# One explicit order for the first 640 steps of a fused windowed-attention and FFN kernel

## The chip, the cores and the metric

The kernel runs on one core of one Trainium2 chip. The metric is device microseconds of one execution, from start to end. Three runs of the kernel before were made, and the median counts. Below, TensorE is PE in the profile's rows (its weight loads are PEld), VectorE is DVE, ScalarE is ACT, GpSimd is POOL and SyncE is SP. A `q` behind a name (SPq, ACTq) means that the engine's queue issued a DMA.

## The reference

Attention with a window of 64 positions over 8 batches, 8 heads, 576 positions of 64 dimensions; its output, as 4608 tokens of 512 numbers, goes through a two-layer network with a leaky rectifier. All in float32.

```python
scores = scale * np.matmul(q, k.transpose(0, 1, 3, 2))
rel = pos[:, None] - pos[None, :]
mask = (rel >= 0) & (rel < window)
scores = np.where(mask, scores, -1000000000.0)
scores = scores - np.max(scores, axis=-1, keepdims=True)
attn = np.exp(scores)
attn = attn / (np.sum(attn, axis=-1, keepdims=True) + 1e-09)
...
h = x @ w_in
g = np.maximum(0.01 * h, h)
return (g @ w_out).astype(np.float32)
```

## The kernel before, in words

Tokens are cut into 9 chunks of 512. Each chunk is 8 units of 64 queries, and two units (one `m`) go through attention together. Products that need full precision are made of three fp32r matmuls: a high and a low part of each operand, without low times low. The first three chunks go through the network as plain matrix products, the other six in three pairs of chunks by a scheme with seven products in place of eight.

The program is one long list of small steps. Each engine executes its own instructions in the order in which the steps were emitted (lines 1514 to 1523 pin that order), and waits at each instruction until its operands are there and its output buffer is free. So the emission order is the order of every queue.

Before the change the emission order has two parts. **ORDER** (line 141) names 514 steps of the head: chunk 0 and most of chunk 1 with the attention they need, and the preparation of weight tiles 0 to 28. They are emitted at once by lines 617 to 619. Then the rest of the kernel is written as a plan, `plan`, of 2303 numbered steps (`op`, line 625), and `arrange` (line 643) emits them in the order of **PLACES** (line 62). A name in ORDER is a kind and a number; `acts`, in front of `step` (line 613), says which function it calls:

- Attention of `m`, or of its half `b` = 2m or 2m+1: `q`, `k`, `v` load from HBM on SP. `S` makes the scores on TensorE (line 369; with the mask, line 403, for all but m = 0), `Z` adds the mask behind S0. `E` copies scores from PSUM to SBUF (line 413 on VectorE for b = 0 and 1, line 415 on ScalarE for the others), `P` takes the maximum over partitions on POOL (line 423, about 2 us), `N` (TensorE, line 437, b < 4) or `sub` (VectorE, line 428) subtracts it, `exp` follows on ScalarE (lines 442 and 444). `V` multiplies by the values (TensorE, line 458), `sm`, `rec` and `y` (VectorE, lines 465, 470, 477) divide by the sum. `T` turns the pair of halves (TensorE, line 484), `H` and `L` split it into high and low part (ScalarE, line 488, and VectorE, line 492).
- Weight half tile `n` (an even n is w_in, an odd one w_out, of tile n // 2): `raw` loads it (SP for n < 3, else the ACT queue), into one of 3 buffers. `bits`, `sign`, `clamp`, `join` on VectorE (lines 317, 321, 329, 334) and `abs` on ScalarE (line 325, between sign and clamp) make it a float32 in one of 2 buffers `w`; `chi` (ScalarE, line 337) makes the high part and issues its store to `w_single` on the ACT queue (line 338); `rest` (VectorE, line 342) makes the low part.
- FFN job `n`: `M` is the first product (TensorE, line 522), `lk` and `gh` the rectifier and the high part (ScalarE, lines 527 and 532), `gl` the low part (VectorE, line 536), `W` the second product (TensorE, line 558). Jobs 0 to 5 are on half a chunk, 256 columns; the others on 512. `ev` copies sums out.
- `X` with a number issues that many dummy 128x512 matmuls on TensorE (`idle`, line 591).

Of the plan's numbers that stand among the first steps: 30 and 31, 44 and 45, 51 and 52 are the first product of later jobs (`early_first`, line 1028), 53 to 56 a second product (`early_second`), 43, 50, 61 its VectorE step `low_of`, 38 to 40 the three stores of weight tile 6 and 46 to 91 other such stores (`store`, line 588, on SP), 149, 164, 179 scores of later `m`, 152 to 170 their POOL reductions.

Around 350 us, in code outside the changed lists, the seven-product stage prepares sums of weights and stores them to `w_sums` from the ACT queue (line 1162); rows below show one ScalarE wait for such a store.

Of the kernel before, what the change touches and what calls it, by code (L numbers as in the profile page):

```python
# [61 lines left out]
PLACES = """  # L62
30 1 7 40 0 38 39 5 2 31 3 10 32 17 41 42 43 44 13 33 34 4 6 45 35 36 9 51 8 12 11 14 15 52 48 16 18 23 49 53 19 59 20 149 50 22 54 21 162
25 55 24 26 56 27 62 28 60 29 63 37 521 46 150 520 61 152 64 69 151 57 65 47 66 155 67 73 153 154 156 164 70 158 71 74 531 165 177 72 530
75 80 522 81 524 76 157 166 167 159 77 68 78 525 523 84 160 526 85 163 82 527 86 91 87 83 170 161 529 88 58 528 89 168 179 532 169 534 173
95 202 181 92 180 96 171 533 172 97 102 182 93 101 98 174 192 535 99 94 536 197 175 193 194 541 540 103 100 537 106 104 185 198 176 105
538 107 183 222 539 108 186 117 184 196 109 178 188 195 204 114 110 206 226 111 205 119 115 543 189 210 217 120 542 544 218 207 116 121
219 127 118 122 187 545 211 203 123 551 190 124 546 130 550 128 131 547 208 191 132 549 199 133 209 134 129 548 220 213 212 221 228 140
146 136 141 135 138 275 142 229 200 143 552 276 147 139 231 137 241 214 554 277 283 555 553 278 251 215 230 556 279 148 280 561 242 246
243 560 223 232 216 234 286 145 227 112 224 557 284 287 235 245 201 288 294 244 289 225 559 233 290 285 271 237 291 247 297 558 295 253  # L70
562 266 236 564 565 298 267 239 603 296 268 238 255 299 125 305 254 300 563 301 566 302 256 240 308 306 567 570 252 309 307 259 571 568
248 310 569 316 257 269 605 270 260 258 79 311 249 607 262 261 312 627 313 319 317 618 318 320 264 606 263 581 619 620 321 327 322 580 250
323 272 324 265 608 273 315 330 572 573 331 611 609 332 341 274 304 333 610 126 612 328 623 343 614 329 622 613 344 621 334 303 624 574
# [123 lines left out]
def band_attention_ffn(ctx: ExitStack, tc: tile.TileContext, qk, vW, vL, w_in, w_out, eye_mask, out, outT):  # L197
# [413 lines left out]
    nc.scalar.copy(unit, eye_in)  # L611

    def step(name):
        kind = name.rstrip("0123456789")
        return partial(acts[kind], int(name[len(kind) :]))

    order, late = ORDER.split("|")
    for name in order.split():
        step(name)()
    prev = jobs[-1]  # L620


    plan = []
# [952 lines left out]
```

## Time and profile before

| what | us |
|---|---|
| median of 3 runs | 841.18 |
| lowest and highest | 840.93, 842.61 |
| span of the profiled execution | 841.2 |
| TensorE busy in it | 829.1 |
| VectorE busy | 630.8 |
| POOL busy | 381.5 |
| ScalarE busy | 369.7 |

The profiled execution is one more run of the same program; the trace gives its own time as the span, 841.2 us from the first to the last instruction. The profile says of each engine when it was busy, and of each idle stretch which other instruction or DMA ended it. A busy TensorE is not TensorE at its peak: matmuls overlap, so a step's cost is read from the distance of starts or from a group's whole time, not from the mean of one matmul.

### The profile page before, as it was taken

How to read it: one execution, taken by the hardware profiler on the slowest of the kernel's cores; microseconds unless marked ns; L12 is line 12 of the kernel's file. 1: busy time of each engine (PE TensorE's matmuls, PEld its weight loads, DVE VectorE, ACT ScalarE, POOL GpSimd, SP SyncE). 2: the span in 40 equal slices, each digit the busy share in tenths (PEclk: the TensorE clock that was granted, in tenths of full speed). 3: DMA queues.
4: the chain of work that ended last, by engine and by line, in shares of the span. 5: the costliest groups of instructions: out<-in, count | busy, mean ns of one | idle time of the engine just before them, and what ended most of it. 6: DMA issues, size and time to landing. Idle time of an engine off the chain costs nothing.

```text
span 841.2 us, 16743 instructions
## 1 busy us (share of the span) xinstructions
PE 829.1 (99%) x6733; PEld 678.1 (81%) x6733; DVE 630.8 (75%) x912; ACT 369.7 (44%) x599; POOL 381.5 (45%) x216
## 2 busy tenths in 40 slices
PE   8999999999999999989999999999999999999997
PEld 5777888888888888868888888887888888888886
DVE  6999897777766698667888987559799863366773
ACT  4666555344423355243564442233545422325432
POOL 5332000897867747687672116797941111111110
PEclk9999999999999999999999999999999999999999
DMA  9886866987887899999999798899998996677772
GB/s 327 278 276 209 310 223 225 319 287 259 277 295 251 271 342 379 365 299 359 361 321 308 224 316 251 255 282 241 261 278 243 317 257 184 190 197 200 212 200 89
DMA packets 131005, 225.75 MB, mean 268 GB/s; under 512 B 15856, under 2 KB 53744, under 8 KB 130928
## 3 DMA queue, kind: packets, MB, share of 16 engines
q0 software_dynamic: 53568, 88.09, 38.8%
q10 hardware_dynamic: 36608, 78.26, 27.6%
q1 hardware_dynamic: 40752, 58.34, 21.7%
q8 instruction: 53, 0.87, 0.4%
q14 instruction: 24, 0.20, 0.1%
HBM read 167.28 MB, written 57.26 MB: 267 GB/s over the span
## 4 chain that ended last, share of the span: by engine, by line
PE 89%; DMA 5%; DVE 3%; issue 1%; ACT 1%; POOL 0%; DVEq 0%; ACTq 0%
PE z L1309 27%; PE m L1243 25%; PE acc L1047 11%; PE h L1038 11%; PE acc L558 4%; PE s L369 4%; PE h L522 4%; PE o L829 3%; DMA w_sums<-pspare 2%; DMA qk<-qk 1%; DMA raw<-w_in 1%; DMA raw<-w_out 1%; DMA w_single<-w 1%; PE o L458 0%; DVE raw L321 0%
## 5 line engine op out<-in xcount | busy, mean ns | idle before, releaser
L1243 PE MATMUL m<-pfew,p 128*128 128x512 f32 x720 | 171.6, 394 | 3.0 <-ACT pxa L1249 2.5
L1243 PEld LDWEIGHTS m<-pfew,p 128*128 128x128 f32 x720 | 135.5, 189 | 32.5 <-ACT pxa L1249 2.9
L1309 PE MATMUL z<-gs,p 128*128 128x512 f32 (+1 forms) x360 | 86.0, 387 | 0.0
L1047 PE MATMUL acc<-p,gs 128*128 128x512 f32 x324 | 80.7, 393 | 0.0
L1309 PE MATMUL z<-pxa,p 128*128 128x512 f32 x324 | 78.5, 391 | 0.0
L1309 PEld LDWEIGHTS z<-gs,p 128*128 128x128 f32 x360 | 67.3, 188 | 13.9
L1309 PE MATMUL z<-pspare,p 128*128 128x512 f32 x324 | 78.0, 389 | 0.0
L1252 DVE TENSOR_TENSOR pxa<-m,pxa 128x512 f32<-128x512 f32 x60 | 41.2, 688 | 48.5 <-PE m L1243 43.6
L770 POOL PARTITION_ALL_REDUCE g<-late_f x20 | 36.3, 1842 | 86.6 <-DVE late_f L755 71.5
L1227 POOL DMA_DIRECT2D p<-w_first x42 | 31.7, 755 | 93.7 <-PE m L1243 51.6
L1309 PEld LDWEIGHTS z<-pspare,p 128*128 128x128 f32 x324 | 60.7, 188 | 12.6
L1309 PEld LDWEIGHTS z<-pxa,p 128*128 128x128 f32 x324 | 60.5, 188 | 12.9 <-issue 0.2
L1243 PE MATMUL m<-pxb,p 128*128 128x512 f32 x288 | 70.6, 391 | 0.0
L1047 PEld LDWEIGHTS acc<-p,gs 128*128 128x128 f32 x324 | 60.0, 188 | 12.8
L773 POOL PARTITION_ALL_REDUCE late_o<-late_f x20 | 65.2, 3274 | 9.6 <-ACT late_f L781 7.4
L773 POOL PARTITION_ALL_REDUCE late_o<-e x18 | 61.5, 3432 | 16.6 <-issue 7.9
L1252 DVE TENSOR_TENSOR p<-m,pxa 128x512 f32<-128x512 f32 x60 | 40.7, 687 | 36.6 <-PE m L1243 35.9
L773 POOL PARTITION_ALL_REDUCE late_o<-late_e x18 | 59.3, 3321 | 10.6 <-ACT late_e L781 6.0
L1243 PEld LDWEIGHTS m<-pxb,p 128*128 128x128 f32 x288 | 53.8, 188 | 11.4
L1227 POOL DMA_DIRECT2D p<-w_sums x24 | 18.0, 749 | 93.1 <-PE z L1309 76.8
L1038 PE MATMUL h<-pxa,p 128*128 128x512 f32 x228 | 55.9, 392 | 0.0
L1038 PEld LDWEIGHTS h<-pxa,p 128*128 128x128 f32 x228 | 42.4, 188 | 9.0
(201 smaller groups left out, 1600.5 us busy)
## 6 DMA issues: line engine op xcount, KB each, us to landing
p<-w_first POOLq DMA_DIRECT2D x42, 1024.0 KB, 7.0
p<-w_sums POOLq DMA_DIRECT2D x24, 1024.0 KB, 6.7
p<-w_second POOLq DMA_DIRECT2D x18, 1024.0 KB, 6.9
qk<-qk ACTq DMA_DIRECT2D x26, 512.0 KB, 6.2
w_single<-w ACTq DMA_DIRECT2D x32, 256.0 KB, 3.7
raw<-w_out ACTq DMA_DIRECT2D x15, 512.0 KB, 4.5
raw<-w_in ACTq DMA_DIRECT2D x14, 512.0 KB, 4.3
more_v<-vL ACTq DMA_DIRECT2D x14, 512.0 KB, 6.0
```

The costliest lines, as they stand in the source:

```text
L369: nc.tensor.matmul(ps[j][t, c : c + QB], k[i][s, p], q[s, w, p], start=not begun and (not more or (w, p) == (0, 0)), stop=not begun and no ...
L522: nc.tensor.matmul(ps, a[:, k, :], b[:, k, part], start=n == 0, stop=n == len(terms) - 1)
L558: nc.tensor.matmul(acc[c, i], a[:, ts], b, start=begin and n == 0, stop=end and n == 2)
L770: nc.gpsimd.partition_all_reduce(most_of(j), e_of(m)[:, j], P, ReduceOp.max)
L773: nc.gpsimd.partition_all_reduce(sum_of(j), e_of(m)[:, j], P, ReduceOp.add)
L829: nc.tensor.matmul(ps[64 * j : 64 * j + 64, c : c + QB], v[:, 2 * p + j], e_of(m)[:, j, c : c + QB], start=True, stop=True,)
L1038: nc.tensor.matmul(ps, a[:, k, :], b[:, k], start=i == 0, stop=i == len(terms) - 1)
L1047: nc.tensor.matmul(acc[c, i], a[:, i * P : (i + 1) * P], b, start=begin and k == 0, stop=n in ends and k == 2)
L1227: nc.gpsimd.dma_start(to, of, max_dma_last_dim=2048)
L1243: nc.tensor.matmul(tiles[b], w[:, 256 * i + 128 * kt : 256 * i + 128 * kt + 128], x_part(OF_X[k], j, kt), start=begin and c == 0, stop=c = ...
L1252: nc.vector.tensor_tensor(to(), tiles[b], x(), ALU.add)
L1309: nc.tensor.matmul(tiles[b + i][:, cut], a, x[:, cut], start=begin and f == first and c == 0, stop=f == half - 1 and c == 2, skip_group_ch ...
```

## The change

PLACES goes. ORDER now holds all 2817 steps, head steps by name and plan steps by number, and `arrange` emits both kinds in that order. The first 640 steps (up to about 170 us of the profile before) stand in a new order; the rest is the order of before. Every step is there once, as it was. The two bookkeeping edits (`turns_late` for `turns`, `room_of` for `more`) keep buffers the same now that head steps are emitted after the plan is written. The steps beyond the common point are cut from the diff.

```diff
--- before.py
+++ after.py
...
-PLACES = """
-30 1 7 40 0 38 39 5 2 31 3 10 32 17 41 42 43 44 13 33 34 4 6 45 35 36 9 51 8 12 11 14 15 52 48 16 18 23 49 53 19 59 20 149 50 22 54 21 162
...
+ORDER = """
+raw0 X6 q1 X2 X1 X2 S0 E1 k1 raw1 E0 Z1 P1 Z0 bits0 S1 sign0 N1 abs0 v0 clamp0 E2 q2 bits1 sign1 P0 join0 exp1 N0 exp0 abs1 P2 E3 clamp1
+k2 raw2 V1 V0 v1 join1 S2 sm0 chi0 sm1 E4 k3 N2 rec1 P3 exp2 y1 raw3 N3 rec0 q3 bits2 sign2 chi1 y0 rest0 T0 exp3 E5 rest1 P4 V2 sm2 V3 v2
+sub4 rec2 raw4 y2 H0 v3 P5 exp4 sm3 rec3 y3 S3 abs2 L0 clamp2 k4 T1 join2 H1 sub5 bits3 sign3 V4 chi2 exp5 q4 L1 sm4 k5 E6 raw5 rec4 V5
+sm5 P6 v4 rec5 abs3 y4 E7 y5 M0 rest2 lk0 T2 gh0 bits4 sign4 q5 sub6 H2 P7 gl0 L2 clamp3 M1 exp6 join3 abs4 V6 clamp4 join4 lk1 gh1 raw6
+chi3 sub7 bits5 chi4 W0 rest4 sign5 S4 exp7 V7 sm6 E8 raw7 E9 M2 sm7 rec6 rec7 y6 y7 P8 abs5 gl1 rest3 lk2 T3 sub8 clamp5 W1 H3 exp8 P9 L3
+V8 gh2 join5 chi5 v5 bits6 sign6 M3 rest5 sub9 abs6 raw8 lk3 clamp6 S5 bits7 exp9 sm8 sign7 abs7 gh3 M4 gl2 q6 join6 raw9 clamp7 k6 W2 gl3
+join7 q7 E10 rec8 y8 bits8 chi6 lk4 chi7 W3 raw10 V9 gh4 rest7 P10 gl4 sm9 sign8 abs8 rest6 bits9 rec9 M5 clamp8 W4 join8 sign9 lk5 sub10
+gh5 raw11 M6 chi8 abs9 y9 bits10 gl5 exp10 sign10 rest8 lk6 E11 clamp9 join9 v6 T4 H4 L4 gh6 raw12 W5 P11 V10 sm10 abs10 bits11 sign11
+sub11 abs11 M7 S6 clamp10 chi9 k7 join10 exp11 clamp11 rec10 y10 gl6 raw13 chi10 E12 P12 lk7 rest9 V11 bits12 sm11 rec11 sign12 rest10
+join11 gh7 abs12 raw14 W6 E13 clamp12 sub12 M8 exp12 chi11 y11 gl7 T5 rest11 V12 join12 H5 W7 P13 sm12 sub13 lk8 bits13 rec12 L5 raw15 y12
+S7 chi12 exp13 sign13 gh8 rest12 abs13 bits14 sign14 E14 clamp13 join13 V13 abs14 bits15 M9 39 v7 gl8 clamp14 E15 chi13 sm13 P14 sub14 W8
+join14 rec13 raw16 lk9 gh9 chi14 y13 raw17 sign15 rest14 T6 exp14 rest13 V14 abs15 sm14 gl9 P15 rec14 H6 sub15 clamp15 exp15 y14 join15
+M10 chi15 bits16 raw18 V15 sign16 abs16 sm15 W9 lk10 L6 rest15 rec15 clamp16 q8 y15 gh10 gl10 bits17 join16 T7 sign17 W10 H7 raw19 chi16
+abs17 L7 M11 clamp17 bits18 join17 raw20 chi17 ev0 rest16 sign18 rest17 abs18 bits19 lk11 sign19 clamp18 join18 gh11 raw21 bits20 M12 gl11
+M13 q9 ev1 sign20 abs19 chi18 abs20 clamp19 rest18 lk12 clamp20 join19 gh12 raw22 gl12 join20 bits21 sign21 chi19 bits22 chi20 W11 W12
+raw23 abs21 rest19 lk13 sign22 gh13 clamp21 join21 M14 chi21 gl13 lk14 rest20 bits23 raw24 M15 gh14 sign23 W13 abs22 clamp22 gl14 lk15
+join22 rest21 M16 abs23 gh15 clamp23 chi22 bits24 sign24 rest22 abs24 join23 raw25 40 chi23 gl15 lk16 rest23 clamp24 W14 join24 bits25
+raw26 W15 gh16 raw27 bits26 sign25 M17 gl16 abs25 lk17 M18 clamp25 join25 chi24 bits27 chi25 gh17 30 sign27 sign26 abs26 rest25 rest24
+gl17 raw28 clamp26 join26 abs27 clamp27 lk18 31 38 join27 1 chi26 W16 W17 rest26 gh18 bits28 chi27 gl18 sign28 41 4 0 32 44 2 5 3 6 7 17
+42 10 8 k8 11 15 33 43 45 51 13 9 12 52 34 19 18 20 v8 14 22 35 48 59 36 21 53 49 24 16 23 26 54 55 56 149 50 28 60 25 29 27 62 37 150 63
+162 152 69 61 151 155 520 521 153 64 65 66 67 156 154 73 157 70 74 71 531 75 76 80 164 46 522 530 160 524 77 158 72 159 177 163 78 84 165
+166 170 525 57 167 523 85 81 68 82 526 91 47 86 161 87 83 527 528 58 88 179 168 529 89 532 169 534 173 95 202 181 92 180 96 171 533 172 97
+102 182 93 101 98 174 192 535 99 94 536 197 175 193 194 541 540 103 100 537 106 104 185 198 176 105 538 107 183 222 539 108 186 117 184
+196 109 178 188 195 204 114 110 206 226 111 205 119 115 543 189 210 217 120 542 544 218 207 116 121 219 127 118 122 187 545 211 203 123
...
-ORDER = """
-raw0 k1 X6 S0 q1 E1 X2 Z1 E0 bits0 sign0 Z0 P1 S1 abs0 v0 P0 raw1 clamp0 join0 N1 E3 bits1 exp1 N0 q2 P3 V1 exp0 sign1
-V0 k2 E2 P2 sm0 rec0 S2 sm1 abs1 rec1 chi0 E4 clamp1 N2 q4 rest0 v1 join1 q3 chi1 exp2 y1 y0 rest1 N3 raw2 T0 bits2
-exp3 P4 k3 sub4 V2 raw3 sm2 E5 sign2 H0 V3 abs2 sm3 rec2 P5 rec3 y2 L0 exp4 v2 clamp2 y3 sub5 join2 raw4 S3 X1 T1
-bits3 exp5 H1 V4 E6 V5 chi2 P6 sm4 v3 sign3 L1 sm5 rec4 X2 M0 rec5 y4 k5 y5 rest2 k4 E7 abs3 raw5 clamp3 lk0 bits4
-join3 gh0 T2 gl0 H2 sub6 sign4 L2 abs4 M1 P7 W0 clamp4 exp6 join4 raw6 lk1 v4 S4 sub7 V6 bits5 chi4 exp7 rest4 sm6
-sign5 E8 V7 sm7 rec6 rec7 gh1 y6 chi3 q6 P8 abs5 y7 M2 raw7 gl1 T3 rest3 E9 q5 H3 W1 sub8 lk2 clamp5 exp8 L3 bits6 gh2
-join5 P9 raw8 gl2 chi5 V8 bits7 M3 sign6 rest5 lk3 abs6 gh3 S5 sign7 abs7 M4 clamp6 q7 v5 gl3 W2 join6 lk4 raw9 sub9
-clamp7 M5 bits8 exp9 join7 sign8 gh4 sm8 W3 rec8 E10 y8 chi6 P10 abs8 gl4 clamp8 chi7 rest6 raw10 lk5 sub10 V9 join8
-bits9 gh5 exp10 W4 v6 sm9 sign9 k6 rec9 gl5 M6 y9 T4 V10 chi8 rest8 abs9 raw11 lk6 rest7 bits10 clamp9 M7 gh6 H4 sm10
-sign10 E11 join9 W5 abs10 chi9 rec10 L4 y10 clamp10 bits11 join10 P11 sub11 S6 gl6 raw12 rest9 exp11 sign11 chi10 V11
-E12 raw13 rest10 abs11 lk7 sm11 gh7 rec11 P12 y11 W6 E13 T5 clamp11 bits12 join11 sign12 abs12 H5 raw14 gl7 bits13 k7
-sub12 clamp12 exp12 L5 join12 sign13 M8 chi11 chi12 W7 lk8 P13 rest11 raw15 rest12 sub13 bits14 abs13 S7 clamp13 V12
-sign14 join13 sm12 exp13 rec12 y12 E14 gh8 q9 abs14 M9 gl8 clamp14 v7 V13 W8 P14 raw16 bits15 sub14 join14 sm13 rec13
-lk9 y13 E15 chi14 exp14 chi13 rest14 sign15 T6 rest13 raw17 V14 gh9 P15 sm14 sub15 abs15 clamp15 H6 M10 rec14 gl9
-exp15 y14 k8 join15 L6 bits16 V15 W9 sm15 lk10 sign16 raw18 rec15 chi15 rest15 gh10 y15 T7 gl10 abs16 H7 clamp16
-join16 W10 bits17 L7 M11 raw19 sign17 M12 bits18 abs17 chi16 ev0 clamp17 join17 sign18 raw20 bits19 abs18 lk11 chi17
-sign19 rest16 gh11 clamp18 join18 v8 gl11 bits20 chi18 rest17 raw21 ev1 sign20 lk12 rest18 abs19 clamp19 join19 bits21
-gh12 gl12 M13 W11 raw22 abs20 M14 chi19 lk13 sign21 clamp20 abs21 gh13 W12 join20 gl13 clamp21 raw23 lk14 bits22
-sign22 rest19 chi20 gh14 rest20 M15 W13 abs22 join21 bits23 clamp22 raw24 chi21 sign23 join22 chi22 gl14 M16 raw25 W14
-abs23 rest21 bits24 sign24 lk15 clamp23 abs24 join23 gh15 rest22 gl15 bits25 clamp24 M17 sign25 chi23 raw26 lk16 gh16
-abs25 W15 join24 gl16 M18 chi24 clamp25 raw27 rest23 q8 bits26 sign26 abs26 lk17 join25 chi25 rest24 gh17 clamp26
-join26 gl17 bits27 sign27 raw28 abs27 chi26 W16 rest25 lk18 clamp27 join27 rest26 chi27 gh18 bits28 sign28 gl18 W17
-|
+LATE_WEIGHTS = """
 abs28 raw29 clamp28 join28 bits29 raw30 sign29 rest27 abs29 bits30 chi28 clamp29 sign30 rest28 abs30 join29 clamp30
 raw31 chi29 bits31 sign31 rest29 abs31 join30 clamp31 chi30 join31 rest30 chi31 rest31
 """
@@ -614,10 +610,8 @@
         kind = name.rstrip("0123456789")
         return partial(acts[kind], int(name[len(kind) :]))
 
-    order, late = ORDER.split("|")
-    for name in order.split():
-        step(name)()
     prev = jobs[-1]
+    turns_late = counter(len(jobs))
 
 
     plan = []
@@ -642,7 +636,11 @@
 
     def arrange():
         placed = set()
-        for n in map(int, PLACES.split()):
+        for word in ORDER.split():
+            if not word.isdigit():
+                yield step(word)
+                continue
+            n = int(word)
             assert placed.issuperset(a["n"] for a in plan[n]["after"])
             placed.add(n)
             yield plan[n]["fn"]
@@ -721,7 +719,7 @@
 
 
     weights_of, raw_of, single_of = {}, {}, {}
-    for name in late.split():
+    for name in LATE_WEIGHTS.split():
         kind = name.rstrip("0123456789")
         n = int(name[len(kind) :])
         o = weights_of.setdefault(n, {})
@@ -733,8 +731,8 @@
             "bits": ["raw"], "sign": ["bits"], "abs": ["sign"], "clamp": ["abs"], "join": ["clamp"], "chi": ["join"],
             "rest": ["chi"],
         }[kind]
-        more = [weights_of.get(n - 2, {}).get("rest")] if kind == "join" else []
-        o[kind] = op(engine, us, step(name), *(o.get(b) for b in before), *more, rank=0.3)
+        room_of = [weights_of.get(n - 2, {}).get("rest")] if kind == "join" else []
+        o[kind] = op(engine, us, step(name), *(o.get(b) for b in before), *room_of, rank=0.3)
     all_in = [weights_of[n][k] for n in (28, 29, 30, 31) for k in ("join", "rest")] + [weights_of[27]["rest"]]
     ready = {f: [weights_of.get(2 * f + i, {}).get("rest") for i in range(2)] for f in range(FT)}
 
@@ -1022,7 +1020,7 @@
     walk = [(c, half + k) for c in range(2) for k in range(half)] + [(2, f) for f in turn_of]
     opens = {n for n in range(len(walk)) if not n or walk[n][0] != walk[n - 1][0]}
     ends = {n for n in range(len(walk)) if n + 1 == len(walk) or walk[n][0] != walk[n + 1][0]}
-    pair_at = [pairs_of_g[next(turns) % 2] for _ in walk]
+    pair_at = [pairs_of_g[next(turns_late) % 2] for _ in walk]
     h_of, tiles, stage = {}, {}, {}
 
     def early_first(n, part):
```

The order on one engine is what is left when the other engines' names are struck out. For TensorE the lists begin so:

```
old: X6 S0 X2 Z1 Z0 S1 N1 N0 V1 V0 S2 N2 N3 T0 V2 V3 S3 X1 T1 V4 V5 X2 M0 T2 M1 W0 S4 V6 V7 M2 T3 W1 V8 M3 S5 M4 W2 M5 W3 V9 W4 M6 T4 V10 M7 W5 S6 V11 W6 T5 M8
new: X6 X2 X1 X2 S0 Z1 Z0 S1 N1 N0 V1 V0 S2 N2 N3 T0 V2 V3 S3 T1 V4 V5 M0 T2 M1 V6 W0 S4 V7 M2 T3 W1 V8 M3 S5 M4 W2 W3 V9 M5 W4 M6 T4 W5 V10 M7 S6 V11 W6 M8 T5
```

## Rows read from the trace of the kernel before

**Rows 1.** The page's first part: busy us (share of the span) and instructions by engine.
```profile
PE 829.1 (99%) x6733; PEld 678.1 (81%) x6733; DVE 630.8 (75%) x912; ACT 369.7 (44%) x599; POOL 381.5 (45%) x216
```

**Rows 2.** Five stretches (us): busy us (x instructions) by engine, TensorE's clock, DMA, GB/s.
```profile
4.60:24.53 19.93, 18.32 (x381) 12.02 (x382) 16.56 (x36) 11.29 (x22) 12.34 (x7) 1.00 0.98 358
24.53:60.00 35.47, 34.34 (x439) 28.20 (x439) 32.96 (x77) 22.64 (x45) 12.11 (x6) 1.00 0.85 272
60.00:357.00 297.00, 297.00 (x2736) 243.33 (x2736) 229.89 (x366) 136.21 (x240) 161.18 (x68) 1.00 0.86 286
357.00:361.00 4.00, 1.51 (x7) 0.90 (x6) 0.93 (x2) 2.14 (x4) 1.45 (x1) 0.95 1.17 368
360.70:364.00 3.30, 3.30 (x10) 2.53 (x9) 2.43 (x5) 2.64 (x5) 2.65 (x3) 0.50 0.64 217
```

**Rows 3.** Timeline of TensorE to 62 us: start, us, what, [idle before <-releaser].
```profile
1.45 2.93 PE L594 MATMUL idle<-p 128*128 128x512 f32 x6 [1.45 <-DVE p L605]
4.60 1.61 PE L369 MATMUL s<-qk 64*64 64x64 f32 x64 [0.22 <-DMA qk<-qk]
...
19.58 1.16 PE L369 MATMUL s<-p 64*64 64x64 f32 x64
...
21.87 0.63 PE L484 MATMUL t<-unit,y 128*128 128x128 f32 x4 [0.69 <-DVE y L477]
...
24.53 1.68 PE L522 MATMUL h<-pxa,pfew 128*128 128x256 f32 x12
...
52.14 0.63 PE L484 MATMUL t<-unit,y 128*128 128x128 f32 x4 [0.73 <-DVE y L477]
...
59.94 2.33 PE L558 MATMUL acc<-pfew,gs 128*128 128x512 f32 x9
```

**Rows 4.** Timeline of all engines to 27 us: VectorE and POOL at the start.
```profile
6.29 1.29 DVE L413 SCALAR_TENSOR_TENSOR e<-s,p 128x512 f32<-128x512 f32 x2 [4.90 <-PE s L369]
7.08 1.99 POOL L423 PARTITION_ALL_REDUCE p<-e  x1 [6.64 <-DVE e L413]
...
7.49 0.90 DVE L317 TENSOR_SCALAR raw<-raw 128x512 uint32<-128x512 uint32 x1
...
9.88 0.49 DVE L329 TENSOR_SCALAR raw<-raw 128x512 f32<-128x512 f32 x1 [0.75 <-ACT raw L325]
...
11.26 1.09 DVE L317 TENSOR_SCALAR raw<-raw 128x512 uint32<-128x512 uint32 x1 [0.16 <-DMA raw<-w_out]
...
13.64 0.16 DVE L465 TENSOR_SCALAR sm<-o 128x4 f32<-128x4 f32 x1 [0.57 <-PE o L458]
```

**Rows 5.** Who VectorE waited for to 100 us: us in total, times, longest.
```profile
DVE raw L317 <- DMA raw<-w_out: 4.2, 3, 2.7
...
DVE w L334 <- DMA w_single<-w: 0.9, 1, 0.9
```

**Rows 6.** Timeline of TensorE, 60 to 130 us.
```profile
77.94 0.69 PE L458 MATMUL o<-p,e 128*64 128x65 f32 x16
...
88.17 8.32 PE L522 MATMUL h<-pxb,pfew 128*128 128x512 f32 x36
```

**Rows 7.** Timeline of VectorE at 27 to 30 us, whose starts give the spacings.
```profile
27.46 0.42 DVE L536 TENSOR_TENSOR gs<-g,gs 128x256 fp32r<-128x256 f32 x1
27.80 0.68 DVE L428 TENSOR_TENSOR e<-e,g 128x512 f32<-128x512 f32 x1
28.40 0.69 DVE L321 SCALAR_TENSOR_TENSOR raw<-raw 128x512 uint32<-128x512 uint32 x1
...
29.83 0.43 DVE L329 TENSOR_SCALAR raw<-raw 128x512 f32<-128x512 f32 x1
```

**Rows 8.** Timeline of the SP queue: the issue of v7.
```profile
70.88 0.55 SPq L266 DMA_DIRECT2D p<-vW  x1
```

**Rows 9.** DMA issues to 100 us: count, KB each, median us to landing.
```profile
p<-vW SPq DMA_DIRECT2D x4, 520.0 KB, 6.3
```

**Rows 10.** Who ScalarE waited for between 350 and 361 us.
```profile
ACT late_f L761 <- DMA w_sums<-pspare: 8.5, 1, 8.5
```

## What the change will do to the time

> **What bounds the kernel now.** I began with the page's line of busy engines: TensorE is busy 829.1 of the span's 841.2 us [rows 1]. Only what TensorE waits for can move the end. Next came the table by stretches [rows 2]: in 4.60 to 24.53 TensorE is busy 18.32 of 19.93 us, in 24.53 to 60 it is busy 34.34 of 35.47, from 60 to 357 all 297.00. So the changed stretch (steps up to about 170 us) has 1.61 + 1.13 = 2.74 us of visible waiting, all of it before 60. After 60 nothing is to be had unless a new wait appears. The timeline of TensorE shows where the early waits lie [rows 3]: S0 starts at 4.60 on a load, T1 comes at 21.87 after 0.69 us on a `y`, M0 at 24.53, T4 at 52.14 after 0.73 on another `y`. The `y` come from VectorE, which is busy 32.96 of those 35.47 us [rows 2]: until 60 the kernel is bound by VectorE's order and TensorE's order together. VectorE itself waits where rows 4 show: 0.75 us for ScalarE before clamp0, 0.16 for a load before bits1, 0.57 for V0 before sm0; later 0.9 for a `w_single` store to land before join8, and 4.2 for three `w_out` loads [rows 5]. Of the 4.2, 0.16 is bits1's and 2.7 belongs to a load behind 60, so 1.3 is left, raw7's. The profile's own span, 841.2 us, stands at the median of the runs (841.18), so I add to that.
>
> **The change part by part.** The work is the same on every engine; only queues are reordered. Four of the moves matter.
>
> *Five dummy matmuls move to the front.* Old: X6, S0, X2, and later X1 before T1 and X2 before M0. New: X6 X2 X1 X2 all ahead of S0. The old ones stood inside waits (X2 ran while VectorE worked on E1, X1 ahead of T1's wait), so taking them out frees nothing. In front they stand in S0's way. Six take 2.93 us from 1.45 [rows 3], ending 4.38. The price of five more has two bounds: 0.23 each by the 36 matmuls of 8.32 us in rows 6, or 2.93 / 6 = 0.49 each. TensorE reaches its higher speed inside S0: S0's 64 small matmuls take 1.61 us, S3's take 1.16 [rows 3]. I take three at 2 x 0.23 and two at 0.23, 1.85 us less some overlap, 1.75: S0 begins at 6.1 where it began at 4.60, runs at full speed, 1.16 + 0.07, and E1 begins at 7.35 where it began at 6.29. That is +1.05 (bounds: start 5.5 to 6.8, so +0.5 to +1.8). The page's granted clock says 1.00 from the start, so this slow phase is read from durations alone.
>
> *VectorE's and ScalarE's order up to M0.* VectorE's work ahead of M0's last need (L1) is the same within one step: with the start-to-start spacings of rows 7 (0.60 for a step on 512 columns that is not a clamp or bits, 0.34 for those and for half-width ones, 0.33 for a `y`, 0.1 for `sm` and `rec`) I sum 13.6 us old and 13.5 new: 15 steps of 0.60, 7 of 0.34, 4 `y`, 8 or 9 small ones. What differs are waits. New: abs1 stands behind exp0 on ScalarE, and exp0 needs N0, N0 needs P0; POOL's two first reductions take about 1.99 us each, back to back behind E1 [rows 4], so they end near 12.1, N0 13.2, exp0 13.9, abs1 14.6, and clamp1 waits about 1.05 us for it. The old wait of 0.57 before sm0 goes, sm0 now comes after join1. rest1 waits about 0.7 for chi1 and clamp2 about 0.65 for abs2, both behind an exp on ScalarE. But L0 and clamp2 (0.94 us) moved from before y3 to behind it, so T1 still comes at about 22.1, against 21.87. Behind T1, clamp2, join2 and sub5 stand ahead of bits3 and L1: L1 ends at about 25.75, and M0 starts there, +1.2 against 24.53.
>
> One price here rests on POOL. bits0 takes 0.90 and bits1 1.09 us while POOL's reductions run [rows 4]; a clamp away from them takes 0.43 [rows 7]. I keep the long prices for the same two steps, since the reductions shift with them; each further step that comes to lie beside a reduction would cost 0.47 to 0.66 more (rival D). The Trainium skill ("GPSIMD Engine Reference", section 1, "Specifications") says that GpSimd shares its SBUF interfaces with VectorE and that VectorE instructions in a two-port mode or with two SBUF inputs contend with it. By that rule `rest` steps too could become long ones, and the sum would be D's; the trace agrees on bits0 and bits1.
>
> *From M0 to T4.* Both orders put the same VectorE steps ahead of sub7 (20.1 us), y7, gl1, sub8 and L3 (25.2 us by the spacings), so the lag stays what it is at M0: M2 comes near 34.4, W2 near 43.1. Then W3 and V9 run ahead of M5 in place of behind it, which moves no sum. T4 needs y9: 37.5 us of steps new, 37.2 old. The old T4 stood 0.73 us idle [rows 3], while VectorE had waited 1.3 us for raw7's load and 0.9 before join8 [rows 5]. raw7 is now issued right behind E8, where gh1, chi3 and abs5 stood between, so its wait goes; the one at join8 stays, as w6's store is issued about as much later. I get y9 at about 52.3 and TensorE ready at about 52.3. **The lag of 1.2 us has shrunk to about 0.2, as the old pauses before T4 are filled.**
>
> *From T4 to 60.* W5 now stands before V10. V11 needs y10 out of the same bank, which now stands behind clamp10, join10, clamp11 on VectorE; it lands near 59.3, V11 near 59.5. W6 needs gl6: 44.8 us of steps against 43.9, W6 near 60.2 where it was at 59.94. From there TensorE is full, as before. Sum: +0.3 us, 841.5.
>
> *The loads' queue.* Step 39 (a store of weight tile 6, waiting for rest12 on VectorE, near 70.6) now stands ahead of v7 on SP; v7 was issued at 70.88 behind q9 and is now issued near 71.1 [rows 8]. Its kind lands after 6.3 us [rows 9], so 77.4; V14 reads it at 77.94 old [rows 6], near 77.9 new. Price: nothing by that row, but with only 0.5 us to spare; a second store of the same queue ahead of it could cost up to 1 us. The other steps beyond it (W's and M's swapped with each other up to 128 us, plan steps by a few places up to 170) move where TensorE has whole stretches queued, 297.00 of 297.00 us [rows 2]. That queue is the cover; if it went, a swapped W would wait for its `gl`, 0.6 us each.
>
> **The rivals.**
>
> A, *slower by the clock*. Between 357 and 361 TensorE waits 2.49 us (busy 1.51 of 4.00), and the granted clock then stands at 0.50 from 360.7 to 364 [rows 2]: half of the 2.4 GHz level, 1.2. Without the X's ahead of T1 and M0, the new order leaves TensorE only V4 and V5 between T1 at 22.1 and M0 at 25.8, with a gap of about 1.8 us. If that brings the same 3.3 us at half speed, M0, T2 and M1 lose about 1.7 us; VectorE waits for gl0 and L2 behind them, and about 1.5 of it stays to T4: 843.0. Against: pauses of 0.69 and 0.73 us [rows 3] brought no such row: the clock reads 1.00 up to 60. It decides if the gap has the effect of the one at 357. Chance 0.11.
>
> B, *slower by the lag*. The 1.2 us at M0 isn't filled before T4, because the `w_single` store that join8 waits for lands one to two microseconds later than in rows 5's case and y9 with it: T4 then waits again, 842.4 to 843.9. For: VectorE is full there. Against: the store is issued no closer to join8 than before. Chance 0.14 for over 0.2%.
>
> C, *faster*. VectorE loses its waits for raw7 and join8 (2.2 us), so TensorE loses the 1.13 us of waiting in 24.53 to 60, the 0.69 before T1 and the 0.69 of X1 and X2 (three at 0.23): 2.5, less what S0's lag leaves, 0.2 to 0.5: about 2.2 off, 839.0. Against: y9 has as many steps ahead as before. Chance 0.12.
>
> D, *steps beside POOL*. Two more bits, clamp or rest steps ahead of L1 fall beside a reduction: 2 x 0.47 to 0.66, so 1.1 more at M0, 842.6 if none of it is absorbed. For: VectorE's order against POOL's is new. Against: the number of reductions and of steps is the same, so others come free. Chance 0.06, inside 0.2%.
>
> E, *the pocket at 357 moves*. It stems from a ScalarE queue that sat 8.5 us behind one `w_sums` store [rows 10], in code the change doesn't touch, but the transfers around it are timed by the shift. If the 2.49 us and half of the 3.3 at 0.50 go, that is -4.1: 837.4; it could also grow by 2. Chance 0.06 for going, 0.04 for growing. That the change does nothing at all can't be, since every queue's order is pinned.
>
> **How the numbers follow.** The three runs spread over 1.7 us, and 0.2% (1.7 us) is about what a measurement of this kernel can tell from no change. Forecast, at 841.5 and within 839.8 to 842.9: 0.47; with D's 0.06 that is 0.53 for no measurable change. Faster by more: C and E, 0.18. Slower by more: A, B and E's growing, 0.11 + 0.14 + 0.04 = 0.29. The range 839.0 to 843.9 holds the forecast, C's centre and A's, and leaves out E and the far ends, some 0.2.
>
> **What would show it.** In the new timeline: S0 at 6.1 and E1 at 7.3; clamp1 waiting for abs1 near 14; M0 near 25.8; T4 near 52.3 with little idle; V11 and W6 at 59.5 and 60.2; TensorE full from there to the pocket at 357, which looks the same. S0 near 4.6, a granted clock of 0.50 between 20 and 40, idle TensorE between 60 and 80, or another pocket would each make it wrong.

## The result, and the profile after

The kernel after takes 853.12 us (median of 4 runs, 850.03 to 856.69) where the kernel before, run beside it, takes 841.89 (4 runs, 840.93 to 843.77). The ratio is 1.014, with a 95% interval of 1.011 to 1.017: slower, and outside the predicted range of 839.0 to 843.9. The profiled execution has a span of 851.8 us, 10.6 over that of before.

After has four or two lines fewer ahead of each function, so L365, L399, L454, L590 answer to L369, L403, L458, L594, and L1036, L1045 to L1038, L1047. The page's first part for after:

```profile
PE 833.0 (98%) x6733; PEld 680.3 (80%) x6733; DVE 631.7 (74%) x912; ACT 370.1 (43%) x599; POOL 378.7 (44%) x216
```

No engine has more work than in [rows 1] that could fill 10.6 us: TensorE is busy 3.9 us longer and idle for the rest. Where, the table by stretches of after tells:

```profile
4.60:28.70 24.10, 21.35 (x381) 13.80 (x381) 17.05 (x34) 11.26 (x22) 12.07 (x7) 1.00 0.85 286
28.70:65.02 36.32, 34.44 (x443) 28.25 (x439) 34.11 (x79) 23.79 (x47) 11.31 (x7) 1.00 0.83 269
65.02:150.00 84.98, 84.98 (x550) 69.69 (x548) 73.46 (x141) 50.35 (x87) 7.93 (x4) 1.00 0.74 240
150.00:182.00 32.00, 26.53 (x284) 21.69 (x283) 17.63 (x25) 8.51 (x14) 23.01 (x10) 0.95 0.78 261
171.10:174.50 3.40, 2.96 (x67) 2.68 (x68) 1.48 (x4) 1.21 (x2) 1.99 (x1) 0.50 1.05 416
```

The first two are [rows 2]'s first two, cut at M0 and W6; the stretch to M0 is 4.17 us longer. From W6 to 150 TensorE is full, as predicted. Then 5.47 us are missing in 150 to 182, and the granted clock stands at 0.50, 1.2 GHz, for 3.4 us right behind. The timeline of TensorE in after, up to W6:

```profile
1.45 6.34 PE L590 MATMUL idle<-p 128*128 128x512 f32 x11 [1.45 <-DVE p L601]
7.72 1.99 PE L365 MATMUL s<-qk 64*64 64x64 f32 x64
...
25.73 0.63 PE L480 MATMUL t<-unit,y 128*128 128x128 f32 x4 [0.28 <-DVE pxa L488]
...
28.09 0.69 PE L454 MATMUL o<-v,e 128*64 128x65 f32 x16 [1.11 <-ACT e L440]
28.70 1.87 PE L518 MATMUL h<-pxa,pfew 128*128 128x256 f32 x12
...
56.46 0.63 PE L480 MATMUL t<-unit,y 128*128 128x128 f32 x4 [0.59 <-DVE y L473]
...
64.40 0.69 PE L454 MATMUL o<-p,e 128*64 128x65 f32 x16 [0.79 <-ACT p L333]
```

Against [rows 3]: S0 is 3.12 us late, T1 3.86, M0 4.17, T4 4.32, and W6, at 65.02, 5.08. The second loss is at the scores of m = 10 (step 179; 9 and 10 below are these m). First TensorE in before, where the scores of 9 and of 10 are the rows of L369, then in after:

```profile
151.29 0.65 PE L369 MATMUL s<-qk 64*64 64x64 f32 x32
...
158.81 2.88 PE L1047 MATMUL acc<-p,gs 128*128 128x512 f32 x12
162.09 0.69 PE L369 MATMUL s<-qk 64*64 64x64 f32 x34
```

```profile
159.07 0.65 PE L365 MATMUL s<-qk 64*64 64x64 f32 x32
...
163.86 2.20 PE L1045 MATMUL acc<-p,gs 128*128 128x512 f32 x9
171.54 0.37 PE L365 MATMUL s<-qk,qk 64*64 64x64 f32 x2 [5.47 <-DMA qk<-qk]
```

In before 9.7 us of other matmuls lie between the two scores (151.94 to 161.69), in after 6.3 (159.72 to 166.06): the new order puts 9 (step 164) behind 74, 75 and 76 and 10 ahead of 89. Between them the load of q and k for 10 (step 177, ScalarE's queue) must land, into the buffer that 9 has just read. The chain that ended last in after tells why it came later still:

```profile
155.76 6.46 POOL late_o L771 x2
162.22 0.02 issue
162.24 0.54 SPq L782
162.78 0.05 issue
162.83 2.37 DMA w_first<-p
165.20 0.02 issue
165.22 0.02 ACTq L258
165.24 0.04 issue
165.28 6.13 DMA qk<-qk
171.40 0.14 issue
171.54 1.99 PE s L365 x64
```

POOL sums m = 8's second half (step 160) ahead of the first (158), so SP's copy of the first sum (159) waits until 162.24, the weight stores behind it on SP wait too, and the load on ScalarE's queue is not issued until the first of these stores has landed. The two have no data in common. What they share is a completion semaphore: the trace shows that SP's and ScalarE's DMAs count on eight of them in turn, that a DMA waits until the one before it on its semaphore has landed, and that this store and this load both use number 108. (Of such pairs, 467 have both times in the trace of after; in none did the later DMA start before the earlier had landed.) ScalarE, behind the load, stands still: its largest wait of that stretch is

```profile
ACT h L1050 <- DMA w_first<-p: 10.1, 1, 10.1
```

For all kernels below, one table of their profiled executions: the starts of S0 and W6 on TensorE, the time from W6 to step 98 (a second product behind all moved steps), and from there to the last matmul. Beside each name stands the ratio of its time to runs of before on the same chip; before took 838.5 to 839.9 there, against 841.89 above, so ratios are compared and not medians.

| kernel | ratio (95%) | S0 | W6 | W6 to 98 | 98 to end |
|---|---|---|---|---|---|
| before | 1 | 4.60 | 59.94 | 106.31 | 670.67 |
| after | 1.0140 (1.0107 to 1.0173) | 7.72 | 65.02 | 113.16 | 669.32 |
| e1 | 1.0105 (1.0061 to 1.0148) | 4.65 | 61.15 | 113.68 | 666.57 |
| e2 | 1.0078 (1.0051 to 1.0105) | 6.87 | 64.10 | 108.38 | 665.44 |
| e3 | 1.0052 (1.0026 to 1.0077) | 4.69 | 60.95 | 107.84 | 667.46 |
| e4 | 1.0010 (0.9982 to 1.0038) | 6.93 | 60.47 | 106.37 | 665.86 |
| e5 | 1.0008 (0.9987 to 1.0029) | 4.63 | 60.35 | 106.35 | 672.20 |
| e6 | 1.0114 (1.0088 to 1.0140) | 7.72 | 65.08 | 110.64 | 667.70 |
| e7 | 1.0042 (1.0018 to 1.0066) | 4.45 | 60.45 | 109.36 | 670.01 |
| e8 | 0.9979 (0.9961 to 0.9997) | 4.52 | 58.72 | 106.33 | 666.24 |
| e9 | 1.0041 (1.0026 to 1.0056) | 4.74 | 61.28 | 107.99 | 668.95 |
| e10 | 0.9993 (0.9979 to 1.0007) | 7.15 | 61.07 | 106.32 | 665.96 |
| e11 | 1.0106 (1.0084 to 1.0128) | 6.46 | 62.00 | 108.02 | 672.19 |
| e12 | 1.0045 (1.0030 to 1.0060) | 4.64 | 60.64 | 108.96 | 666.96 |
| e13 | 1.0046 (1.0022 to 1.0070) | 4.67 | 61.18 | 106.81 | 666.38 |
| e14 | 1.0111 (1.0080 to 1.0142) | 7.72 | 64.08 | 106.40 | 672.95 |
| e15 | 1.0062 (1.0038 to 1.0086) | 5.53 | 62.49 | 108.35 | 666.20 |
| e16 | 1.0075 (1.0048 to 1.0102) | 7.72 | 64.26 | 107.29 | 666.19 |

So after loses 5.08 us up to W6 and 6.85 from W6 to 98, and regains 1.35 behind, where the pocket at 357 of [rows 2] is smaller: +10.6 in all. A part of this table is chance: with one and the same head, before, e5, e7 and e8 have W6 at 58.72 to 60.45.

### The profile page after: what moved, and what is told of

The parts are those of the page before. It is cut to its first block, busy times and chain, and to the rows that moved or that the text cites. A ratio compares the mean times of both kernels' runs of the same rounds, so it can differ in the third digit from the quotient of the medians.

```text
span 851.8 us, 16734 instructions
## 1 busy us (share of the span) xinstructions
PE 833.0 (98%) x6733; PEld 680.3 (80%) x6733; DVE 631.7 (74%) x912; ACT 370.1 (43%) x599; POOL 378.7 (44%) x216
## 4 chain that ended last, share of the span: by engine, by line
PE 87%; DMA 5%; DVE 4%; issue 2%; POOL 1%; ACT 1%; ACTq 0%; SPq 0%; POOLq 0%; DVEq 0%
PE z L1307 27%; PE m L1241 24%; PE acc L1045 9%; PE h L1036 9%; PE acc L554 4%; PE s L365 4%; PE h L518 4%; PE o L827 3%; DMA qk<-qk 2%; DMA w_sums<-pspare 1%; DMA w_single<-w 1%; POOL late_o L771 1%; PE idle L590 1%; DVE w L330 1%; DVE raw L317 1%
## 5 line engine op out<-in xcount | busy, mean ns | idle before, releaser
L1045 PE MATMUL acc<-p,gs 128*128 128x512 f32 x324 | 81.5, 395 | 0.0
L1045 PEld LDWEIGHTS acc<-p,gs 128*128 128x128 f32 x324 | 60.2, 189 | 12.9
L771 POOL PARTITION_ALL_REDUCE late_o<-late_f x20 | 64.6, 3249 | 10.2 <-ACT late_f L779 8.6
L1036 PE MATMUL h<-pxa,p 128*128 128x512 f32 x228 | 55.7, 392 | 0.0
L1036 PEld LDWEIGHTS h<-pxa,p 128*128 128x128 f32 x228 | 42.5, 188 | 9.1
```

Of the source, the lines that this page charges most:

```text
L771: nc.gpsimd.partition_all_reduce(sum_of(j), e_of(m)[:, j], P, ReduceOp.add)
L1036: nc.tensor.matmul(ps, a[:, k, :], b[:, k], start=i == 0, stop=i == len(terms) - 1)
L1045: nc.tensor.matmul(acc[c, i], a[:, i * P : (i + 1) * P], b, start=begin and k == 0, stop=n in ends and k == 2)
```

## The experiments

### The wait at the scores of m = 10

**e2**: the pair of sums put back in after.

```diff
-522 530 160 524 77 158 72
+522 530 158 524 77 160 72
```

> The new order with POOL's two sums of m = 8 in the old sequence (158 ahead of 160); nothing else differs. Theory: compact_of8,0 on SP waits for the sum that POOL now makes second, the stores behind it on SP wait too, and the load of qk for m = 10 waits for one of these stores, since it takes the semaphore that the store releases. Then TensorE's 5.5 us wait near 170 goes, with the half-speed stretch behind it, and the time falls by 5 to 7 us, to about 847. Rival: that load is late because it is issued late in the new order or because the head lags; then the wait stays over 3 us and the time over 850.

Measured: 846.56 (843.72 to 850.05, 8 runs). The wait of 5.47 is down to 1.31 and W6 to 98 to 108.38: the turned pair is needed for 4.78 of the 6.85 us. What is left is the same thing, only shorter. The scores of 9 end at 158.94, and still the load is issued 2.6 us later, when the SP store before it on semaphore 109 has landed (161.49); it lands after 5.46 us, at 167.03, and the scores of 10 start at 167.16:

```profile
161.57 0.34 ACTq L258 DMA_DIRECT2D qk<-qk  x1
```

**e5**: the kernel before with the pair turned.

```diff
-156 164 70 158 71
+156 164 70 71
...
-157 166 167 159 77 68 78 525 523 84 160 526
+157 160 158 166 167 159 77 68 78 525 523 84 526
```

> The kernel before, with one thing of the new order: POOL's second sum of m = 8 (step 160) stands ahead of its first (158), as after. The load of q and k of m = 10 (step 177, ScalarE's queue) stays ahead of both, where the order of before has it. If the wait of 5.47 us near 170 comes only when that load is queued behind a store of SP that is itself queued behind SP's copy of the first sum (159), this kernel has no such wait: the load is issued near 152 and TensorE is full from 150 to 180; time within 1.5 us of before. If the turned pair of sums alone is the cause, TensorE waits some 5 us near 165 to 172 and the granted clock falls behind it: 845 or more, 5 to 7 over before.

Measured: 840.50, as before. POOL's two sums and the load in its timelines:

```profile
151.99 0.34 ACTq L262 DMA_DIRECT2D qk<-qk  x1
```

```profile
155.22 6.54 POOL L773 PARTITION_ALL_REDUCE late_o<-late_f  x2 [5.95 <-ACT late_f L781]
```

The sums are as late as in after, and nothing is lost (106.35): the load was out 3 us before they began. The pair alone is harmless.

**e6** and **e11**: in after, the load moved up, first a little, then far.

```diff
-159 177 163
+159 163
...
-522 530 160
+177 522 530 160
```

```diff
-159 177 163
+159 163
...
-67 156 154 73 157 70 74 71 531 75 76 80 164 46
+67 73 74 75 76 164 177 156 154 157 70 71 531 80 46
```

> The kernel after, with the turned pair of sums left as it is; only step 177, the load of q and k of m = 10, moves up on ScalarE's queue, ahead of a load of weights (530). If the queue is the cause, the load is issued near 156 instead of 165, TensorE does not wait 5.47 us near 170, no half clock follows, and the time falls by 5 to 7 us against after, as it did with the pair turned back (846.6): 846 to 848. If the late sum itself or SP's late stores are what TensorE waits for, the wait stays at 4 us or more or moves to another operand, and the time stays within 2 us of after's 853.1.

> The kernel after with the turned pair of sums kept; the load of q and k of m = 10 (177) moved further than in e6: ahead of ScalarE's exps of m = 8, with TensorE's four steps that it follows. There it no longer counts on the completion count that SP's copy of the late sum (159) uses. If the shared count is the cause, the load is issued near 152, no wait and no half clock come at 165 to 175, and the time is 845.5 to 847.5, as in e2 with the pair turned back. If the late sum costs time of itself, TensorE waits 2 us or more near 165 to 172 for something else, and the time is 849 or more.

Measured: 849.87 and 849.27, both above what the theory expected. In e6 the load took the semaphore of SP's copy itself and was issued when that had landed. The queues of SP and ScalarE, then TensorE:

```profile
162.34 0.54 SPq L782 DMA_DIRECT2D late_c<-late_o  x1
```

```profile
164.14 0.36 ACTq L258 DMA_DIRECT2D qk<-qk  x1
```

```profile
169.47 0.27 PE L365 MATMUL s<-qk,qk 64*64 64x64 f32 x2 [3.30 <-DMA qk<-qk]
```

Issued 1.14 us earlier, a wait 2.17 shorter, and no half clock behind it. In e11 it no longer shared with SP's late transfers, but then waited for the scores of 9, and with it ScalarE's exps:

```profile
156.31 0.34 ACTq L258 DMA_DIRECT2D qk<-qk  x1
...
156.70 1.15 ACT L779 ACTIVATE late_f<-late_f 128x512 f32<-128x512 f32 x2 [10.47 <-PE s L365]
```

TensorE's wait for the load was gone, but TensorE now waited 1.43 us at 159.73 for a low part (gs, L1056) that came late in turn, and 1.97 at 181.5 with half clock behind it. A load can't be moved ahead of what frees its buffer; it only stops its own queue.

**e14**: in after, the scores of 9 and the load both where before has them; the pair stays turned.

```diff
-67 156 154 73 157 70 74 71 531 75 76 80 164 46
+67 156 154 73 164 157 70 74 71 531 177 75 76 80 46
...
-159 177 163
+159 163
```

> The kernel after with 164 and 177 alone put where the order of before has them; the pair of sums stays turned and the dummies stay in front. If the place of 164, which lets the load be issued only after it, is half of the cause and the late sum the other half, curing this half alone is enough: the load is issued before SP's copy of the late sum comes into its way, near 152 to 156, TensorE does not wait 2 us or more between 160 and 175, and the time is 845 to 848, as in e2, where the other half was cured. If the turned pair costs by itself, a wait of that size stays and the time is 849 or more.

Measured: 848.54 (845.78 to 852.75, 6 runs), half a microsecond over what was expected. TensorE, ScalarE's queue and POOL:

```profile
155.50 0.68 PE L365 MATMUL s<-qk 64*64 64x64 f32 x32
...
165.64 0.69 PE L365 MATMUL s<-qk 64*64 64x64 f32 x34
```

```profile
156.25 0.36 ACTq L258 DMA_DIRECT2D qk<-qk  x1
```

```profile
154.99 6.45 POOL L771 PARTITION_ALL_REDUCE late_o<-late_f  x2 [1.48 <-ACT late_f L779]
```

The load is issued right behind the scores of 9, ahead of SP's late copy; TensorE does not wait, and W6 to 98 is 106.40, as before. So all 6.85 us need both halves: the scores of 9 moved back on TensorE with the load behind them, and the turned pair on POOL. The first half without the second costs 1.0 to 2.6 (W6 to 98 is 107.29 to 108.96 in e2, e3, e12, e15 and e16), the second without the first nothing (e5). This is read from the profiles; the ratios of e14 and after, 1.0111 and 1.0140, have intervals that overlap. That e14's time did not fall by all of the 6.85 us is due, in this profile, to a pocket at 365 to 375 (98 to end 672.95), the old one of [rows 2] come back: TensorE waits 1.05 and 1.77 us there, and the clock is at 0.50 for 3.4.

### What the numbered steps still cost

**e7**: the head of before, the numbered steps in the order of after with the pair put back.

```diff
-30 1 7 40 0 38 39 5 2 31 3 10 32 17 41 42
+39 40 30 31 38 1 41 4 0 32 44 2 5 3 6 7
...
```

**e9**: e3 (below) with e11's edit and e8's (below). **e13**: e3 with e14's edit and e8's.

> The head in the order of before with its dummy matmuls in their old places; the plan's numbered steps in the order of after, with 158 ahead of 160. It tells where the 4.8 us lie that were left with both cures (844.6 against 839.9). If the numbered steps hold them (TensorE's waits of 1.23 us near 163, 0.52 near 339 and 1.24 near 366 in that kernel), this one stands 2.5 to 4.5 us over before and shows those waits. If the new head holds them (V11 and W6 1 us late, weights' steps later behind it), it is within 1 us of before, and TensorE is full at 163.

> The kernel after with four mends at once: the dummy matmuls X2, X1, X2 back in their old places, 158 ahead of 160, the load of q and k of m = 10 (177) moved up ahead of ScalarE's exps of m = 8, and the second weight-sum store near 349 us (1214) moved as in the mended kernel of before (e8). If the numbered steps' waits near 163 and 350 to 370 are what was left of the loss, TensorE is full at 163 and from 330 to 400, and the time is 838 to 840.5: about 1 us over e8's 837.8, for V11 and W6. If the new order costs something that no such wait shows, it stays at 842 or more.

> The kernel after with the dummies and the pair of sums put back (e3) and the mend near 349 us (e8), and two steps more put where the order of before has them: TensorE's scores of m = 9 (step 164) ahead of 74, 75 and 76, and the load of q and k of m = 10 (177), which needs the buffer that those scores free, behind 531. In e9 the load was moved alone: it still had to wait for 164, and ScalarE stood still behind it. If the place of 164 is the root, the load is issued near 151 to 153, no wait of 1.2 to 1.5 us comes near 160, and the time is 838.5 to 841, some 2 to 4 under e3 and e9. If the waits near 160 are due to something else (weights' steps running late), one of a microsecond or more is still there and the time stays at 842 or more.

Measured: e7 843.47, with waits of 0.85 at 138.7 and 1.41 at 164.5 and W6 to 98 3.0 over before's: most of e3's remaining loss lies in the numbered steps. e9 842.52: the wait moved to 159.0 (1.43, the low part again), so the mend did not mend it. e13 842.18 (839.49 to 850.32, 12 runs): no wait is left near 160, and W6 to 98 is 106.81, within 0.5 of before; the root of that wait is the place of the scores of 9, with the load. Its time is still 1.2 us above what was expected. By its profile, 1.2 us lie ahead of W6 and 0.5 behind; the rest of its 3.7 over before is in runs that no profile shows, and stays open.

### The dummy matmuls

**e1**: after with X2, X1, X2 back. **e3**: e1 and e2. **e12**: e2 without them. **e15**: e2 with all eleven in one group. **e16**: e2 again.

```diff
-raw0 X6 q1 X2 X1 X2 S0 E1 k1 raw1 E0 Z1
+raw0 X6 q1 S0 E1 k1 raw1 E0 X2 Z1
...
-k4 T1 join2
+k4 X1 T1 join2
...
-y5 M0 rest2
+y5 X2 M0 rest2
```

```diff
-raw0 X6 q1 X2 X1 X2 S0
+raw0 X11 q1 S0
```

**e4**: before with the three in front, as after. **e10**: e8 with the same.

```diff
-raw0 k1 X6 S0 q1 E1 X2 Z1
+raw0 k1 X6 X2 X1 X2 S0 q1 E1 Z1
...
-S3 X1 T1
+S3 T1
...
-rec4 X2 M0
+rec4 M0
```

> The new order with X2, X1 and X2 back in their old places (behind S0, ahead of T1, ahead of M0); nothing else differs. Theory: the five dummies ahead of S0 make the lag of the head. Then S0 starts near 4.6 us, W6 near 60 (65.0 in the new kernel, 59.9 in the old one), the wait for a qk load near 170 stays at 5 us or so, and the time falls by 4 to 5 us, to about 848.5. Rival: the lag comes from the new order of VectorE and ScalarE; then W6 stays at 64 or later and the time stays over 851.

> Both edits on the new order. If the two theories hold and add up, about 842, within 1.5 us of the kernel before; the 640 steps' other moves then cost or give no more than that. Rival: the rest of the new order costs something of its own; then over 844.

> The kernel before, with X2, X1 and X2 moved ahead of S0, nothing else. Theory: S0 starts near 7.7 us and at half speed, as in the new kernel, and the time rises by 3.5 to 5 us, to about 846. Rival: the dummies cost only in company of the new order; then within 1.5 us of the kernel before.

> The mended kernel of before (e8) with X2, X1, X2 in front of S0 as after. On a base without the pocket near 357, the price of the dummies alone: by the prediction's step S0 starts 1.5 us late and T4's old idle time takes most of it, +0.3 to +0.6 at W6, 838.1 to 838.6. If they cost what they seem to cost in the kernel after (4.5 us between after and e1), 841 or more, with TensorE at half clock until 14 us.

> The kernel after with 158 ahead of 160 (e2), without X2, X1, X2 anywhere: X6 alone in front. Against e2's 846.6. If the place in front of S0 is what costs, S0 starts at 4.6, M0 near 25.6, and the time falls by about 2 us, to 844.6, as with the dummies back behind S0 (e3). If what costs is that no dummies stand ahead of T1 and M0, so that TensorE's pauses there bring the granted clock of 0.50 (e2 had it at 25.9 to 29.3), it stays at 846 or more and shows that clock between 20 and 40 us.

> The kernel after with 158 ahead of 160 (e2), its eleven dummy matmuls in front of S0 as one group X11 in place of X6, X2, X1, X2. In the trace of after the second group starts only when the first has ended (4.43 after 4.38, 5.71 after 5.66, 6.57 after 6.51), so each group costs a drain. If these drains are what holds S0 back and keeps TensorE at 1.2 GHz until 14 us in some runs, S0 starts at 5.8 to 6.6, the full clock comes by 6 us, the runs lie closer together, and the median is 1 to 2 us under the run of e2's kernel beside it, near e12's 844.2. If the number of dummies in front of S0 is the cost, it stays within 0.7 us of that kernel.

> The kernel of e2 once more, beside e15 on the same chip: X6, X2, X1, X2 in front of S0 and the pair of sums put back. By the earlier run 846.6. Its profile is a second look at the start: if the late full clock (14.1 us in after, 14.4 in e6, 10.2 in e14, 5.4 in e2, 4.5 in e11) changes from one execution to the next, it may differ from e2's; if it went with the order of the steps, it is 5.4 again and S0 starts near 6.9.

Measured: e1 848.63 (with the wait at the scores of 10 still there, 5.13 us), e3 844.64, e4 840.98, e10 838.83 (e8, the same without, 837.83), e12 844.19, e15 844.53, e16 844.43. In the old order the three groups cost about 1 us by the medians, inside the intervals (0.9993 for e10, 0.9979 for e8); the 3.5 to 5 us expected of e4 did not come. In the new order, with the pair put back, they cost some 2 to 3: ratios of 1.0078 and 1.0075 (e2, e16) against 1.0052 behind S0 (e3) and 1.0045 without them (e12), intervals that overlap too. W6 says the same: 60.64 to 61.28 in the five kernels with the new head and nothing more in front, 62.00 to 65.08 in the seven that have them there.

The front of e15, then of e11:

```profile
1.45 4.15 PE L590 MATMUL idle<-p 128*128 128x512 f32 x11 [1.45 <-DVE p L601]
5.53 1.16 PE L365 MATMUL s<-qk 64*64 64x64 f32 x64
```

```profile
1.45 5.08 PE L590 MATMUL idle<-p 128*128 128x512 f32 x11 [1.45 <-DVE p L601]
6.46 1.16 PE L365 MATMUL s<-qk 64*64 64x64 f32 x64
```

Eleven dummies in one group end 1.22 us later than the six of [rows 3]; in four groups, 2.15 in e11 and 3.41 in after and e16. In e15 and e11 S0 takes 1.16 us, so TensorE was at full speed: the three further drains alone cost about 0.93. The other 1.26 in after are a slow start: its S0 takes 1.99 us, and the trace's record of the full clock begins at 14.1 us there and at 10.3 in e16, against 4.4 and 4.5 in e15 and e11. That is not a matter of the order: e16 is e2 again, and in e2 that record begins at 5.4, with S0 at 6.87 and 1.16. Between 25 and 30 us it went the other way: e2, which was fast early, had the half clock there, e16 did not. e2's table by stretches:

```profile
20.00:25.90 5.90, 4.18 (x121) 3.33 (x122) 5.62 (x14) 4.21 (x9) 1.95 (x2) 1.00 0.94 308
25.90:29.30 3.40, 3.40 (x27) 3.28 (x28) 3.28 (x11) 1.52 (x3) 1.78 (x1) 0.50 1.03 364
```

e15 has the same at 24.9 to 28.3. So e15's earlier S0 was given back, and its median is e16's, where 1 to 2 us less were expected: the drain between groups is shown, but as the price of the dummies in the whole kernel it is not. Both kernels have W6 late, by 2.5 and 4.3 us. e12 and e11 had the same two pauses ahead of that place (0.61 and 1.11 us) and kept the full clock, so what decides between them stays open.

### The pocket at 357, and a kernel that beats both

**e8**: the kernel before, the second of two `w_sums` stores (step 1214) moved behind the load of q and k for m = 24 (841).

```diff
-799 1214 800
+799 800
...
-1296 1235
+1296 1214 1235
```

> The kernel before, with the second of two stores of weight sums near 349 us (step 1214, ScalarE's queue) moved behind the load of q and k of m = 24 (841) and seven more ScalarE steps, up to just ahead of the weight load that needs its buffer. In the profile of before that load waited until 358.35 for the first such store to land, 14.6 us after its issue, and TensorE then waited 2.49 us and ran 3.4 us at the granted clock of 0.50. If the shared completion count is the cause, the load is issued near 350.4, ScalarE has no wait of 8 us, the pocket is gone in every run, and the median is 1 to 3 us under before's. If the store only takes the place of the load as the one that waits, or the weight load behind it comes late, it is within 1 us of before or over it.

Measured: 837.83 (837.20 to 840.68, 12 runs) against 839.59 of before (836.35 to 843.78, 29 runs): ratio 0.9979, 0.9961 to 0.9997, the only kernel here below 1 by its interval. The load in before and in e8:

```profile
358.42 0.34 ACTq L262 DMA_DIRECT2D qk<-qk  x1
```

```profile
352.21 0.37 ACTq L262 DMA_DIRECT2D qk<-qk  x1
```

It no longer shares a semaphore with the store of [rows 10]. ScalarE still has an idle stretch of 6.27 us there, so that part of the expectation was wrong, but TensorE's waits from 60 to 400 come to 0.2 us, and 98 to end to 666.24 where before has 670.67. (Its W6, 1.22 us earlier than before's, has nothing to do with the edit.) Its 12 runs reach up to 840.68, those of before to 843.78. It is the same mechanism as at 171 in after, and it was in the kernel before the change.

How much it costs changes from one execution to the next. e4 has the order of before around 357, and there the load is held by the same store too, but the store landed 10.2 us after its issue and not 14.6:

```profile
354.59 0.34 ACTq L262 DMA_DIRECT2D qk<-qk  x1
```

TensorE did not wait, no half clock came, and 98 to end is 665.86. So one profile without the pocket does not show that the edit removed it; what shows a gain is the median, by 0.2%.

## Why the prediction was wrong

**The step that failed most** is the one on the steps beyond 60 us: "move where TensorE has whole stretches queued ... That queue is the cover". It costed the numbered steps up to 170 at nothing; in the profile of after they cost 6.85 us (113.16 against 106.31, and 106.40 in e14, which moves two of them). A full queue covers a late operand only as far as the distance to its use. Two moves on TensorE cut the distance for the load of 10 from 9.7 to 6.3 us, of which the load itself takes 5.46 (e2) to 6.13 (after). Moved behind steps of SP, the load then had to wait for an SP store by way of a shared semaphore, 2.6 us in e2; the pair turned on POOL made that 5.6 in after. The prediction had named a pocket's pattern in [rows 10], a ScalarE queue behind one store, and gave it a place only at 357 (rival E). That one was 1.35 smaller, which may be chance, as e4 shows; a new one of the same kind was the case left out.

**The dummies.** The prediction put S0 at 6.1 (5.5 to 6.8) and E1 1.05 late; S0 came at 7.72 and E1, at 9.77, 3.48 late. The mis-sized term is "three at 2 x 0.23 and two at 0.23", 1.85 us: it measures 3.41 in after. The drains between the groups, 0.93 (e11 against e15), were not in the sum, and the full speed that the sum had from S0 on came later: S0 took 1.99 in place of 1.16.

**The lag up to T4** was to shrink from 1.2 us at M0 to 0.2; it went from 4.17 to 4.32. In e11, the kernel nearest to the sum's start (E1 1.40 late), it went from 1.47 to 1.31. The term that failed is VectorE's wait of 1.3 for raw7's load, struck out as gone. It was gone, but bits9 now waited for its own load, raw9, ahead of the wait at join8:

```profile
52.66 0.43 DVE L313 TENSOR_SCALAR raw<-raw 128x512 uint32<-128x512 uint32 x1 [1.01 <-DMA raw<-w_out]
...
54.08 0.69 DVE L330 SCALAR_TENSOR_TENSOR w<-raw 128x512 uint32<-128x512 uint32 x1 [0.59 <-DMA w_single<-w]
```

e3 has M0 at 25.56 and T4 at 52.39, close to the sum's 25.8 and 52.3. That is luck: the sum had E1 1.05 late, and in e3 it is 0.17 late.

**From T4 to W6** the sum had 7.9 us (52.3 to 60.2). It is 7.80 in before and 8.55 or 8.56 in all twelve kernels with the new head. V11 waits for y10, as the sum had it: y10's signal comes 0.14 us before V11 starts. (The row of V11 at 64.40 names ScalarE's chi10, L333, but the signal of that step comes no sooner than V11 starts.) y10 is late because join9, a step costed at 0.60 from start to start, took 1.41, where such a step elsewhere takes 0.69, beside a reduction of POOL that began at 58.26:

```profile
58.56 1.41 DVE L330 SCALAR_TENSOR_TENSOR w<-raw 128x512 uint32<-128x512 uint32 x1
...
63.83 0.42 DVE L473 TENSOR_TENSOR y<-o,sm 128x256 f32<-128x256 f32 x1
```

**What held.** v7 and V14 cost nothing: V14 starts at 83.00, late by 5.06, just as W6. TensorE was full from W6 to 150.

**The rivals.** A, the half clock after the pauses at T1 and M0, is real: e2 and e15 show it, 3.4 us long as at 357; after itself does not. B had it right that the lag would not be filled before T4, but not why: join8 waits 0.59 us in after, less than the 0.88 of before. C did not happen: VectorE still waits 1.0 us for a load and 0.8 for stores on that stretch. D happened in part, in steps with two SBUF operands: beside reductions, join1 takes 1.53 in after and join9 1.41, against 0.69 for such a step elsewhere. For what D rests on, the Trainium skill ("GPSIMD Engine Reference", section 1, "Specifications") names that very kind. These durations agree, but e3's sign0, of that kind too, takes 0.69 at 8.60 in the middle of a reduction (7.25 to 9.24), so the kind alone does not tell which step becomes long.

## What to carry to other kernels

Before an edit moves steps "under cover", check for each load that must land between two uses of its buffer how much work is left between them, and against it the load's time to landing with whatever may hold up its issue; here 6.3 us of work against 5.5 to 6.1 us of landing left under 1 us, and being held for 2.6 (e2) was enough to make TensorE wait. Then follow what the DMA shares: here a completion semaphore that two engines' queues use in turn made a weight store on SP, held up by a sum on POOL, stop a load on ScalarE's queue, and moving the load a little earlier (e6) only met the next partner. A change that is measured as one number may hold parts that are harmless alone: the turned pair cost nothing in the old order, and nothing was lost with the scores put back.

## What was not expected of the hardware

Dummy matmuls in several groups cost more than their count: five more took 1.22 us in one group (e15) and 2.15 in three further groups at the same speed (e11). How soon TensorE was at full speed changed from one execution to the next: behind the same eleven dummies S0 took 1.16 us in e2 and 1.99 in e16, the same kernel, and behind six it took 1.99 too in e5 and e7, where before has 1.61. Why is open.
